# Grouped-query attention against a cache: wo in 4 KB rows, K four batches ahead from batch 20 on, a second block-diagonal P buffer in place of a ring slot

## The chip, the core and the metric

The kernel runs on one core of one Trainium2 chip. The core has a matrix engine (PE, with its weight loads listed as PEld), a vector engine (DVE), a scalar engine (ACT), a general engine (POOL), a sync engine (SP) whose only work here is to issue transfers, 16 DMA engines, an on-chip memory of 128 partitions (SBUF) and a small accumulator memory (PSUM) that the matrix engine writes. The metric is the device time of one execution in microseconds; several runs are made and the median is compared.

## What is computed

Thirty-two batches with four new tokens each attend to a cache of 2048 keys and values. There are 32 query heads over 4 key/value heads, so 8 query heads share one of K and V.

```python
B, Sq, D = 32, 4, 1024
Hq, Hkv, Sk, Dh = 32, 4, 2048, 128          # all tensors bf16
q = (x @ wq).reshape(B, Sq, Hq, Dh).transpose(0, 2, 1, 3)
k = jnp.repeat(k_cache, Hq // Hkv, axis=1)
v = jnp.repeat(v_cache, Hq // Hkv, axis=1)
scores = jnp.einsum("bhqd,bhkd->bhqk", q, k) * (Dh ** -0.5)
p = softmax(scores, axis=-1)
o = jnp.einsum("bhqk,bhkd->bhqd", p, v)
out = o.transpose(0, 2, 1, 3).reshape(B, Sq, Hq * Dh) @ wo
```

K and V of one batch are 2 MB each, wq and wo 8 MB each: some 151 MB have to be read.

## The kernel before

**Loads.** All large transfers are issued by SP, in one order written out in the code (L159 to L186): x, wq in four pieces, then K and V batch by batch, then wo in ten pieces (`WO`, in heads of 128 rows). The order of K and V is `loads` (L159): K of batches 0 to 2, then for each batch b K of b+3 (`LEAD`) and V of b. A transfer is 2 MB, 16 KB for each partition. They go round a ring of eight slots of 2 MB (`big`, `NS`): a load waits until the load that had its slot eight places before has been used up, that is until the last quarter of its K is transposed (`kt`, chunk 3) or its P*V is done (`pv`). wo goes into four slots of the same ring after the last V, in rows of 2 KB, and each of its pieces waits for its slot in the same way. SP waits in order: what is behind a waiting issue waits too.

**The projection** (L199 to L242) makes Q for all batches and leaves it transposed in `QT_sb`.

**One iteration i of the loop** (L367 to L386) writes, for each engine, its work in program order:

- POOL, `qd` (L254): the queries of batch i+1 are put on a block diagonal, `QD_sb`, four copies.
- DVE, `kt` (L263): K of batch i+1 is transposed in four chunks, two before and two after the maximum of batch i.
- PE, `pe_qk` (L271): 16 matmuls of 512 columns make the scores of batch i in `ps_s`, the one score buffer. They wait for the exp of batch i-1, which reads that buffer.
- DVE, `softmax_max` (L288): the row maximum and its negative. ACT, `softmax_exp` (L293): exp into `P_sb`, with the row sums.
- PE and ACT, `pe_ot` and `ot_evac` (L331, L336) of batch i-3: the scaled output of a batch is transposed by one matmul against the identity and copied to `oT_sb`, which shares its place with `QT_sb`; the heads of a token lie side by side there.
- DVE, `pt` (L299): P is transposed into one of two buffers `PT_sb`.
- PE, `pe_pv` (L317), 64 matmuls, and ACT, `o_evac` (L326): P*V of batch i-2 and its scaling by the inverse row sum.
- POOL, `pd` (L308): P of batch i-1 is put on a block diagonal in `PD_sb` by four copies of 32 partitions. There is one such buffer, so these copies wait for P*V of the batch before. At the end a second one, `PE_sb`, is made out of a buffer of transposed K that is no longer used; ACT zeroes it in iteration 30 (L378), it takes batch 30, and three of the four copies of batch 31 are done by DVE.

After the loop come P*V of batches 30 and 31 with what follows them, then the output product `oproj` (L344): 64 matmuls over wo's heads, in the order of its ten pieces, all of them behind the last `ot_evac`, and the copy and store of the result.

**Order around the change.** Every engine works through its own list in order, with waits on the other engines' counters. PE's list in iteration i is: scores of i, output transpose, P*V of i-2. So a P*V that waits for its V holds back the scores of the next batch.

In the profile, line L16 is the helper that issues a matmul with weights already loaded; such rows belong to the scores, to the projection or to the output product by their tile names.

Of the kernel before, what the change touches and what calls it, by code (L numbers as in the profile page):

```python
# [78 lines left out]
def bass_standalone__gqa_block_cached__sampling_kernel(  # L79
# [21 lines left out]
    NW = 4  # L101
    LEAD = 3
    NC = D // 2
    WO = (4, 4, 4, 4, 4, 4, 4, 2, 1, 1)
# [5 lines left out]
    with ExitStack() as es:  # L110
# [8 lines left out]
        QT_sb = sbuf("QT_sb", [128, B, 2, REP, Sq, 2], BF16)  # L119
        oT_sb = QT_sb[:, :, :, :, :, :].rearrange("p b a h s w -> p (b a h s w)").rearrange("p (t h) -> p t h", h=Hq)  # L120
        QD_sb = sbuf("QD_sb", [128, 2, 2, G, 32, 2], BF16)
# [5 lines left out]
        PD_sb = sbuf("PD_sb", [128, T // 2, G, 32, 2], BF16)  # L127
        PE_sb = KT_sb[:, B % 2, :, :, :, :].rearrange("p t a r w -> p (t a r w)")
        PE_sb = PE_sb.rearrange("p (t g q w) -> p t g q w", t=T // 2, g=G, q=32)
        o_sb = sbuf("o_sb", [128, Dh], BF16)  # L130
        y_sb = sbuf("y_sb", [128, D], BF16)

# [27 lines left out]
        for b in range(B):  # L160
            loads += [("k", b + LEAD)] if b + LEAD < B else []
            loads += [("v", b)]
        slot_of = {}
        holder = {s: "w" for s in range(NW)}
        for n, (kind, b) in enumerate(loads):
            s = (NW + n) % NS
            before, holder[s], slot_of[kind, b] = holder.get(s), (kind, b), s
            waits = [] if before is None else ["qproj"] if before == "w" else [
                ("kt", before[1], NCH - 1) if before[0] == "k" else ("pv", before[1])]
            src = (k_cache if kind == "k" else v_cache)[b].rearrange("g (r t) d -> (g r) t d", r=R)  # L170
            p.dma("sp", lambda e, s=s, src=src: e.dma_start(big[:, s, :, :], src), waits, (kind, b), f"s_b{s}")
        n = len(loads)
        wo_slot = [(NW + n + c) % NS for c in range(NW)]

        def wo_at(h):
            return big[:, wo_slot[h // 8], :, :].rearrange("p t d -> p (t d)")[:, h % 8 * D:(h % 8 + 1) * D]

        h0 = 0
        for c, m in enumerate(WO):
            assert h0 // 8 == (h0 + m - 1) // 8  # L180
            kind, b = holder[wo_slot[h0 // 8]]
            dst = big[:, wo_slot[h0 // 8], :, :].rearrange("p t d -> p (t d)")[:, h0 % 8 * D:(h0 % 8 + m) * D]
            p.dma("sp", lambda e, dst=dst, h0=h0, m=m: e.dma_start(
                dst.rearrange("p (h n) -> p h n", h=m), wo[h0 * 128:(h0 + m) * 128, :].rearrange("(h p) n -> p h n", p=128)),
                [("kt", b, NCH - 1) if kind == "k" else ("pv", b)], ("wo", c), f"s_wo{c}")
# [119 lines left out]
        def pd_of(i):  # L305
            return PE_sb if i == B - 2 else PD_sb

        def pd(i):  # L308
            for g in range(G):
                rows = slice(32 * g, 32 * (g + 1))  # L310
                src = words(PT_sb[rows, i % 2, :, :, :].rearrange("p t q w -> p t (q w)"))
                dst = words(pd_of(i)[rows, :, g, :, :].rearrange("p t q w -> p t (q w)"))
                waits = [("pt", i)] + (["pe0"] if i == B - 2 else ["pd0"] + ([("pv", i - 2 if i == B - 1 else i - 1)] if i else []))
                p.op("dve" if i == B - 1 and g < 3 else "pool", lambda e, s=src, d=dst: e.tensor_copy(d, s),  # L314
                     waits, ("pd", i, g))

# [14 lines left out]
        def pe_ot(i):  # L331
            buf, waits = slot(("ot", i))
            buf = ring_of["ot", i] = buf.bitcast(BF16)
            p.op("pe", lambda e: e.transpose(buf[:, 0:128], o_sb[:, :], ident[:, :]), waits + [("o", i)], ("oT", i))  # L334

        def ot_evac(i):  # L336
            buf = ring_of["ot", i]
            p.op("act", lambda e: e.activation(  # L338
                oT_sb[:, i * Sq:(i + 1) * Sq, :].rearrange("p s h -> p h s"),
                buf[:, 0:128].rearrange("p (h s) -> p h s", s=Sq), ACT.Copy),  # L340
                [("oT", i), ("qd", i)], ("ot", i))


        def oproj(c):  # L344
            for h in range(sum(WO[:c]), sum(WO[:c + 1])):
                for j in range(2):
                    out_, lhsT, rhs = ps_s[:, NC * j:NC * (j + 1)], oT_sb[:, :, h], wo_at(h)[:, NC * j:NC * (j + 1)]
                    if j == 0:
# [17 lines left out]
        kt(0, range(NCH))  # L366
        for i in range(B):  # L367
            if i < L:
                qd(i + 1)
                kt(i + 1, (0, 1))  # L370
            pe_qk(i)
            softmax_max(i)
            if i >= 3:
                pe_ot(i - 3)
                ot_evac(i - 3)
            softmax_exp(i)
            if i == L - 1:
                p.op("act", lambda e: e.memzero(words(PE_sb.rearrange("p t g q w -> p (t g q w)"))), [("qk", i)], "pe0")  # L378
            if i < L:
                kt(i + 1, (2, 3))  # L380
            pt(i)
            if i >= 2:
                pe_pv(i - 2)
                o_evac(i - 2)
            if i >= 1:
                pd(i - 1)  # L386

        pe_pv(L - 1)
        pe_ot(L - 2)
        ot_evac(L - 2)  # L390
        o_evac(L - 1)
        pd(L)
        pe_pv(L)
        pe_ot(L - 1)
        ot_evac(L - 1)
        o_evac(L)
        pe_ot(L)
# [60 lines left out]
```

## Time and profile before

Four runs took 368.52 to 371.19 us, median 370.11. The profiled execution is the one of 371.19 us; its span, from its first to its last instruction, is 369.3 us.

| | before |
|---|---|
| median of 4 runs | 370.11 us |
| profiled execution, its span | 371.19 us, 369.3 us |
| PE busy | 281.4 us (76%) |
| DVE busy | 275.2 us (75%) |
| POOL busy | 164.1 us (44%) |
| ACT busy | 122.9 us (33%) |
| read from HBM | 151.26 MB, 410 GB/s over the span |
| mean granted PE clock | 0.953 |

How to read the page's parts: the slices divide the span into 40 equal stretches of 9.23 us, and each digit is the busy share in tenths (PEclk: the granted clock of PE in tenths of full speed). The chain of work that ended last is followed back from the last instruction; a row of it has its start in us, its duration in us, the engine, what is written and the line. A row of an engine's timeline has start, duration, engine, line, operation, what is written and read, shape and count, and in square brackets how long the engine had stood idle and what ended that. Issues of transfers are listed with the time from issue to landing.

### The profile page before, as it was taken

Reading aid. Unit: us, or ns where it says so; the run is one execution under the profiler, and the core shown is the slowest. Engines: PE = TensorE matmul, PEld = TensorE weight load, DVE = VectorE, ACT = ScalarE, POOL = GpSimd, SP = SyncE. Lnnn points to the kernel's source line nnn. Section 1 sums busy time; section 2 is a strip of 40 time slices with the busy share of each in tenths; the row PEclk is TensorE's granted clock in tenths of the full one; section 3 lists DMA queues with packets and bytes.
Section 4 is the critical chain, followed back from the end, with each engine's and each line's share of the span. In section 5 each row is a group of like instructions: output and inputs, shape, how many; then the busy total and the mean of one; then the engine's idle time right before and its main releaser. Section 6 shows DMA issues by size and latency. Waiting matters only on the chain.

```text
span 369.3 us, 5961 instructions
## 1 busy us (share of the span) xinstructions
PE 281.4 (76%) x2744; PEld 144.8 (39%) x2272; DVE 275.2 (75%) x273; ACT 122.9 (33%) x135; POOL 164.1 (44%) x262
## 2 busy tenths in 40 slices
PE   1973557888888877777888878777878777768796
PEld 1001002444444444444444455433535344455722
DVE  0029577999999999999999987898697998673300
ACT  1020112333344444444433433443143344464200
POOL 5001050555555555555554445555554655518100
PEclk9998678999999999999999989998998999989989
DMA  8999999999999999999999999999999999999991
GB/s 334 431 428 426 429 428 433 431 424 425 421 428 426 426 428 426 432 426 424 428 426 428 428 427 423 426 431 426 428 428 426 428 426 429 422 426 401 387 337 47
DMA packets 14506, 151.90 MB, mean 411 GB/s; under 512 B 1296, under 2 KB 1552, under 8 KB 5776
## 3 DMA queue, kind: packets, MB, share of 16 engines
q1 hardware_dynamic: 14336, 151.39, 97.4%
q8 instruction: 20, 0.33, 0.4%
q10 hardware_dynamic: 144, 0.13, 0.1%
q14 instruction: 6, 0.05, 0.0%
HBM read 151.26 MB, written 0.26 MB: 410 GB/s over the span
## 4 chain that ended last, share of the span: by engine, by line
DMA 34%; PE 31%; DVE 18%; ACT 8%; issue 7%; SPq 1%
DMA big<-in_v_cache_dram 29%; PE ps_s L16 18%; DVE mx L289 12%; ACT P_sb L294 7%; PE ps_s L281 6%; DMA big<-in_wq_dram 6%; PE ps_r L321 5%; DVE KT_sb L269 3%; PE ps_s L349 2%; DVE negmx L290 1%; DVE PD_sb L314 1%; DVE QT_sb L242 1%; DVE KT_sb L226 1%; SPq L156 0%; ACT QT_sb L338 0%
## 5 line engine op out<-in xcount | busy, mean ns | idle before, releaser
L314 POOL COPY PD_sb<-PT_sb 32x1024 f32<-32x1024 f32 x121 | 125.6, 1038 | 136.2 <-DVE KT_sb L269 66.5
L269 DVE STREAM_TRANSPOSE KT_sb<-big 128x1024 f32<-128x1024 f32 x128 | 150.7, 1216 | 6.4 <-DMA big<-in_k_cache_dram 6.1
L321 PE MATMUL ps_r<-big,PD_sb 128*128 128x128 bf16 x1984 | 122.1, 225 | 28.3 <-DMA big<-in_v_cache_dram 25.3
L321 PEld LDWEIGHTS ps_r<-big,PD_sb 128*128 128x128 bf16 x1984 | 117.9, 101 | 35.7 <-POOL QD_sb L260 23.1
L294 ACT ACTIVATE P_sb<-ps_s,negmx 128x2048 bf16<-128x2048 f32 x32 | 81.6, 2550 | 84.4 <-DVE negmx L290 84.4
L16 PE MATMUL ps_s<-KT_sb,QD_sb 128*128 128x512 bf16 x384 | 108.2, 390 | 0.0
L289 DVE TENSOR_REDUCE mx<-ps_s 128x1 f32<-128x2048 f32 x32 | 73.3, 2290 | 22.6 <-PE ps_s L16 22.2
L281 PE MATMUL ps_s<-KT_sb,QD_sb 128*128 128x512 bf16 x128 | 50.1, 392 | 43.9 <-ACT P_sb L294 37.7
L281 PEld LDWEIGHTS ps_s<-KT_sb,QD_sb 128*128 128x128 bf16 x128 | 12.7, 99 | 123.0 <-issue 73.9
L338 ACT ACTIVATE QT_sb<-ps_r 128x128 bf16<-128x128 bf16 x32 | 23.6, 736 | 107.2 <-PE ps_r L334 107.2
L302 DVE STREAM_TRANSPOSE PT_sb<-P_sb 128x1024 f32<-128x1024 f32 x32 | 39.9, 1245 | 14.6 <-ACT P_sb L294 14.6
L260 POOL COPY QD_sb<-QT_sb 32x64 f32<-32x64 f32 x128 | 29.4, 230 | 41.7 <-DVE QT_sb L242 25.4
L357 DVE CAST y_sb<-ps_s 128x512 bf16<-128x512 f32 x1 | 0.7, 692 | 21.4 <-PE ps_s L349 21.4
L226 DVE CAST KT_sb<-ps_r 128x512 bf16<-128x512 f32 x2 | 1.3, 686 | 20.1 <-PE ps_r L210 20.1
L328 ACT ACTIVATE o_sb<-ps_r,rinv 128x128 bf16<-128x128 f32 x32 | 11.9, 371 | 12.1 <-PE ps_r L321 12.1
L349 PE MATMUL ps_s<-big,QT_sb 128*128 128x512 bf16 x32 | 13.2, 411 | 0.9 <-ACT QT_sb L338 0.9
L16 PE MATMUL ps_s<-big,QT_sb 128*128 128x512 bf16 x32 | 13.1, 411 | 0.0
L334 PEld LDWEIGHTS ps_r<-ident,o_sb 128*128 128x128 bf16 x32 | 3.1, 96 | 23.4 <-issue 22.3
L349 PEld LDWEIGHTS ps_s<-big,QT_sb 128*128 128x128 bf16 x32 | 4.7, 146 | 11.4 <-issue 11.3
L16 PE MATMUL ps_s<-big,P_sb 128*128 128x512 bf16 x32 | 9.1, 411 | 0.0
L228 ACT ACTIVATE KT_sb<-ps_r 128x512 bf16<-128x512 f32 x2 | 1.1, 594 | 23.5 <-PE ps_r L16 23.5
L210 PEld LDWEIGHTS ps_r<-big,P_sb 128*128 128x128 bf16 x8 | 0.8, 104 | 19.7 <-issue 11.7
(30 smaller groups left out, 69.0 us busy)
## 6 DMA issues: line engine op xcount, KB each, us to landing
big<-in_k_cache_dram SPq DMA_DIRECT2D x32, 2048.0 KB, 27.8
big<-in_v_cache_dram SPq DMA_DIRECT2D x32, 2048.0 KB, 32.3
big<-in_wq_dram SPq DMA_DIRECT2D x4, 2048.0 KB, 13.9
big<-in_wo_dram SPq DMA_DIRECT2D x7, 1024.0 KB, 19.0
big<-in_wo_dram SPq DMA_DIRECT2D x1, 512.0 KB, 12.8
big<-in_wo_dram SPq DMA_DIRECT2D x2, 256.0 KB, 10.3
P_sb<-in_x_dram SPq DMA_DIRECT2D x1, 256.0 KB, 2.7
out_dram<-y_sb SPq DMA_DIRECT2D x1, 128.0 KB, 1.8
```

The lines of the kernel that those rows point to most:

```text
L16: return eng.add_instruction(mybir.InstMatmult(name=nc.get_next_instruction_name(), engine=eng.engine, start_tensor_calc=start, stop_tenso ...
L260: p.op("pool", lambda e, s=src, d=dst: e.tensor_copy(d, s), waits if g == 0 else [], ("qd", i) if g == G - 1 else None)
L269: p.op("dve", lambda e, s=src, d=dst: e.transpose(d, s), waits, ("kt", i, c))
L281: mm = lambda e, a_=(out_, lhsT, rhs), f=first, l=last: e.matmul(a_[0], lhsT=a_[1], rhs=a_[2], start=f, stop=l, skip_group_check=True)
L289: p.op("dve", lambda e: e.tensor_reduce(mx[:, i % 4:i % 4 + 1], ps_s[:, :], AX.X, ALU.max), [("qk", i)], ("mx", i))
L294: p.op("act", lambda e: e.activation(P_sb[:, :, :, :].rearrange("p t r w -> p t w r"), ps_s[:, :].rearrange("p (t w r) -> p t w r", w=2, r=R),
L302: p.op("dve", lambda e: e.transpose(dst, src), [("exp", i)] + ([("pd", i - 2, G - 1)] if i > 1 else []), ("pt", i))
L314: p.op("dve" if i == B - 1 and g < 3 else "pool", lambda e, s=src, d=dst: e.tensor_copy(d, s), waits, ("pd", i, g))
L321: p.op("pe", lambda e, t=t: e.matmul(buf[:, 0:Dh], lhsT=pd_of(i)[:, t // 2, :, :, t % 2].rearrange("p g q -> p (g q)"), rhs=big[:, slot_of ...
L328: p.op("act", lambda e: e.activation(o_sb[:, :], buf[:, 0:Dh], ACT.Copy, scale=rinv[:, i % 4:i % 4 + 1]), [("pv", i), ("rinv", i)] + ([("o ...
L338: p.op("act", lambda e: e.activation(oT_sb[:, i * Sq:(i + 1) * Sq, :].rearrange("p s h -> p h s"), buf[:, 0:128].rearrange("p (h s) -> p h ...
L349: mm = lambda e, a=(out_, lhsT, rhs), h=h: e.matmul(a[0], lhsT=a[1], rhs=a[2], start=(h == 0), stop=(h == Hq - 1), skip_group_check=True)
```

## The change

- wo is loaded in rows of 4 KB: two neighbouring rows of wo go to one partition. The output therefore has to be transposed with even and odd features apart, and the one matmul of `pe_ot` becomes four with 64 columns of weights each, into halves of the partitions; `oT_sb` becomes a buffer of its own in which the 128 tokens of a weight tile lie side by side. `y_sb`, the result before its store, moves into `P_sb`.
- `SL = 20`: when V of batch 20 is due, K of batches 23 and 24 are loaded ahead of it; from there on K of b+4 is loaded ahead of V of b. From load number 43 (K of 23) on, the ring has seven slots; the eighth, `spare`, becomes `PF_sb`, a second block-diagonal P buffer, zeroed by ACT in iteration 20.
- Batches 21, 23, ..., 31 use `PF_sb`, the others `PD_sb`, and the copies wait for the last P*V that read their buffer. All copies are on POOL.
- `SW = 24`: iteration 24 has no P*V and no output transpose; from iteration 25 on P*V is that of batch i-3. After the loop come P*V of 29, 30 and 31.

```diff
@@ -100,6 +100,8 @@
     NS = 8
     NW = 4
     LEAD = 3
+    SW = 24
+    SL = 20
     NC = D // 2
     WO = (4, 4, 4, 4, 4, 4, 4, 2, 1, 1)
     scale = float(Dh) ** -0.5
@@ -117,7 +119,7 @@
         q_sb = KT_sb[:, 1, :, :, :, :].rearrange("p t a r w -> p (t a r w)")[:, 0:Hq * Dh]
         q_sb = q_sb.rearrange("p (h a g e) -> p h a g e", h=REP, a=2, g=G)
         QT_sb = sbuf("QT_sb", [128, B, 2, REP, Sq, 2], BF16)
-        oT_sb = QT_sb[:, :, :, :, :, :].rearrange("p b a h s w -> p (b a h s w)").rearrange("p (t h) -> p t h", h=Hq)
+        oT_sb = sbuf("oT_sb", [128, Hq // 2, 2, NT], BF16)
         QD_sb = sbuf("QD_sb", [128, 2, 2, G, 32, 2], BF16)
         P_sb = sbuf("P_sb", [128, T // 2, R, 2], BF16)
         P_flat = P_sb[:, :, :, :].rearrange("p t r w -> p (t r w)")
@@ -125,10 +127,8 @@
         xT_sb = P_flat[:, D:2 * D].rearrange("p (a b) -> p a b", b=128)
         PT_sb = sbuf("PT_sb", [128, 2, T // 2, 32, 2], BF16)
         PD_sb = sbuf("PD_sb", [128, T // 2, G, 32, 2], BF16)
-        PE_sb = KT_sb[:, B % 2, :, :, :, :].rearrange("p t a r w -> p (t a r w)")
-        PE_sb = PE_sb.rearrange("p (t g q w) -> p t g q w", t=T // 2, g=G, q=32)
         o_sb = sbuf("o_sb", [128, Dh], BF16)
-        y_sb = sbuf("y_sb", [128, D], BF16)
+        y_sb = P_flat[:, D:2 * D]
 
         ident = sbuf("ident", [128, 128], BF16)
         identf = sbuf("identf", [128, 128], F32)
@@ -158,30 +158,44 @@
 
         loads = [("k", b) for b in range(LEAD)]
         for b in range(B):
-            loads += [("k", b + LEAD)] if b + LEAD < B else []
-            loads += [("v", b)]
+            ahead = [b + LEAD] if b < SL else [b + LEAD, b + LEAD + 1] if b == SL else [b + LEAD + 1]
+            loads += [("k", a) for a in ahead if a < B] + [("v", b)]
+        n_pd = loads.index(("k", SL + LEAD))
+        spare = (NW + n_pd) % NS
+        pd_holder = loads[n_pd - NS]
+
+        def ring_slot(n):
+            if n < n_pd:
+                return (NW + n) % NS
+            return (spare + 1 + (n - n_pd) % (NS - 1)) % NS
+
+        PF_sb = big[:, spare, :, :].rearrange("p t d -> p (t d)").rearrange("p (t g q w) -> p t g q w", t=T // 2, g=G, q=32)
         slot_of = {}
         holder = {s: "w" for s in range(NW)}
         for n, (kind, b) in enumerate(loads):
-            s = (NW + n) % NS
+            s = ring_slot(n)
             before, holder[s], slot_of[kind, b] = holder.get(s), (kind, b), s
             waits = [] if before is None else ["qproj"] if before == "w" else [
                 ("kt", before[1], NCH - 1) if before[0] == "k" else ("pv", before[1])]
             src = (k_cache if kind == "k" else v_cache)[b].rearrange("g (r t) d -> (g r) t d", r=R)
             p.dma("sp", lambda e, s=s, src=src: e.dma_start(big[:, s, :, :], src), waits, (kind, b), f"s_b{s}")
         n = len(loads)
-        wo_slot = [(NW + n + c) % NS for c in range(NW)]
-
-        def wo_at(h):
-            return big[:, wo_slot[h // 8], :, :].rearrange("p t d -> p (t d)")[:, h % 8 * D:(h % 8 + 1) * D]
-
+        wo_slot = [ring_slot(n + c) for c in range(NW)]
+
+        def wo_at(h, m):
+            return big[:, wo_slot[h // 8], :, :].rearrange("p t d -> p (t d)")[:, h % 8 * D:(h % 8 + m) * D]
+
+        wo_v = wo.rearrange("(h p e) n -> p h (e n)", p=128, e=2)
         h0 = 0
         for c, m in enumerate(WO):
             assert h0 // 8 == (h0 + m - 1) // 8
             kind, b = holder[wo_slot[h0 // 8]]
-            dst = big[:, wo_slot[h0 // 8], :, :].rearrange("p t d -> p (t d)")[:, h0 % 8 * D:(h0 % 8 + m) * D]
-            p.dma("sp", lambda e, dst=dst, h0=h0, m=m: e.dma_start(
-                dst.rearrange("p (h n) -> p h n", h=m), wo[h0 * 128:(h0 + m) * 128, :].rearrange("(h p) n -> p h n", p=128)),
+            if m > 1:
+                dst = wo_at(h0, m).rearrange("p (h n) -> p h n", n=2 * D)
+                src = wo_v[:, h0 // 2:(h0 + m) // 2, :]
+            else:
+                dst, src = wo_at(h0, 1), wo_v[:, h0 // 2, h0 % 2 * D:(h0 % 2 + 1) * D]
+            p.dma("sp", lambda e, dst=dst, src=src: e.dma_start(dst, src),
                 [("kt", b, NCH - 1) if kind == "k" else ("pv", b)], ("wo", c), f"s_wo{c}")
             h0 += m
         assert h0 == Hq
@@ -303,16 +317,16 @@
             p.op("dve", lambda e: e.reciprocal(rinv[:, i % 4:i % 4 + 1], ssum[:, i % 4:i % 4 + 1]), [("exp", i)], ("rinv", i))
 
         def pd_of(i):
-            return PE_sb if i == B - 2 else PD_sb
+            return PF_sb if i > SL and i % 2 else PD_sb
 
         def pd(i):
+            free = [j for j in range(i) if pd_of(j) is pd_of(i)]
+            free = ("pv", free[-1]) if free else "pd0" if pd_of(i) is PD_sb else "pf0"
             for g in range(G):
                 rows = slice(32 * g, 32 * (g + 1))
                 src = words(PT_sb[rows, i % 2, :, :, :].rearrange("p t q w -> p t (q w)"))
                 dst = words(pd_of(i)[rows, :, g, :, :].rearrange("p t q w -> p t (q w)"))
-                waits = [("pt", i)] + (["pe0"] if i == B - 2 else ["pd0"] + ([("pv", i - 2 if i == B - 1 else i - 1)] if i else []))
-                p.op("dve" if i == B - 1 and g < 3 else "pool", lambda e, s=src, d=dst: e.tensor_copy(d, s),
-                     waits, ("pd", i, g))
+                p.op("pool", lambda e, s=src, d=dst: e.tensor_copy(d, s), [("pt", i), free], ("pd", i, g))
 
         def pe_pv(i):
             buf, waits = slot(("o", i))
@@ -330,21 +344,26 @@
 
         def pe_ot(i):
             buf, waits = slot(("ot", i))
-            buf = ring_of["ot", i] = buf.bitcast(BF16)
-            p.op("pe", lambda e: e.transpose(buf[:, 0:128], o_sb[:, :], ident[:, :]), waits + [("o", i)], ("oT", i))
+            ring_of["ot", i] = buf
+            for e_ in range(2):
+                for u in range(2):
+                    out_ = buf[64 * u:64 * (u + 1), 64 * e_:64 * (e_ + 1)]
+                    lhsT = o_sb.rearrange("p (d e) -> p e d", e=2)[:, e_, :]
+                    rhs = ident.rearrange("p (h u s) -> p u h s", u=2, s=Sq)[:, u, :, :]
+                    p.op("pe", lambda e, a=(out_, lhsT, rhs): e.matmul(a[0], lhsT=a[1], rhs=a[2], start=True, stop=True),
+                         waits + [("o", i)] if e_ == u == 0 else [], ("oT", i) if e_ == u == 1 else None)
 
         def ot_evac(i):
             buf = ring_of["ot", i]
             p.op("act", lambda e: e.activation(
-                oT_sb[:, i * Sq:(i + 1) * Sq, :].rearrange("p s h -> p h s"),
-                buf[:, 0:128].rearrange("p (h s) -> p h s", s=Sq), ACT.Copy),
-                [("oT", i), ("qd", i)], ("ot", i))
-
+                oT_sb[:, :, :, i * Sq:(i + 1) * Sq].rearrange("p h e s -> p e h s"),
+                buf[:, 0:128].rearrange("p (e h s) -> p e h s", e=2, s=Sq), ACT.Copy),
+                [("oT", i)], ("ot", i))
 
         def oproj(c):
             for h in range(sum(WO[:c]), sum(WO[:c + 1])):
                 for j in range(2):
-                    out_, lhsT, rhs = ps_s[:, NC * j:NC * (j + 1)], oT_sb[:, :, h], wo_at(h)[:, NC * j:NC * (j + 1)]
+                    out_, lhsT, rhs = ps_s[:, NC * j:NC * (j + 1)], oT_sb[:, h // 2, h % 2, :], wo_at(h, 1)[:, NC * j:NC * (j + 1)]
                     if j == 0:
                         mm = lambda e, a=(out_, lhsT, rhs), h=h: e.matmul(
                             a[0], lhsT=a[1], rhs=a[2], start=(h == 0), stop=(h == Hq - 1), skip_group_check=True)
@@ -365,35 +384,34 @@
         qd(0)
         kt(0, range(NCH))
         for i in range(B):
+            j = i - 2 if i < SW else i - 3 if i > SW else -1
             if i < L:
                 qd(i + 1)
                 kt(i + 1, (0, 1))
             pe_qk(i)
             softmax_max(i)
-            if i >= 3:
-                pe_ot(i - 3)
-                ot_evac(i - 3)
+            if j > 0:
+                pe_ot(j - 1)
+                ot_evac(j - 1)
             softmax_exp(i)
-            if i == L - 1:
-                p.op("act", lambda e: e.memzero(words(PE_sb.rearrange("p t g q w -> p (t g q w)"))), [("qk", i)], "pe0")
+            if i == SL:
+                p.op("act", lambda e: e.memzero(words(PF_sb.rearrange("p t g q w -> p (t g q w)"))),
+                     [("kt", pd_holder[1], NCH - 1) if pd_holder[0] == "k" else ("pv", pd_holder[1])], "pf0")
             if i < L:
                 kt(i + 1, (2, 3))
             pt(i)
-            if i >= 2:
-                pe_pv(i - 2)
-                o_evac(i - 2)
-            if i >= 1:
+            if j >= 0:
+                pe_pv(j)
+                o_evac(j)
+            if i > 0:
                 pd(i - 1)
 
-        pe_pv(L - 1)
-        pe_ot(L - 2)
-        ot_evac(L - 2)
-        o_evac(L - 1)
         pd(L)
-        pe_pv(L)
-        pe_ot(L - 1)
-        ot_evac(L - 1)
-        o_evac(L)
+        for j in range(L - 2, L + 1):
+            pe_pv(j)
+            pe_ot(j - 1)
+            ot_evac(j - 1)
+            o_evac(j)
         pe_ot(L)
         ot_evac(L)
         for c in range(len(WO)):
```

## The prediction

> **What bounds the kernel now.** I read the page's slices first, then the chain of work that ended last, then each engine's timeline around it.
>
> ```profile
> PEclk9998678999999999999999989998998999989989
> DMA  8999999999999999999999999999999999999991
> GB/s 334 431 428 426 429 428 433 431 424 425 421 428 426 426 428 426 432 426 424 428 426 428 428 427 423 426 431 426 428 428 426 428 426 429 422 426 401 387 337 47
> ```
>
> The transfer queue is full for nearly the whole span, at about 427 GB/s, a 2 MB load every 4.9 us and an iteration's two loads every 9.8. The drop to 387 comes with wo in its 2 KB rows. So time can only be won after the last load. The chain shows two regimes ahead of that:
>
> ```profile
> 188.05 2.30 DVE mx L289
> 190.56 1.14 ACT P_sb L294
> 191.70 1.27 issue
> 193.29 0.38 PE ps_s L281
> ...
> 326.42 5.36 PE ps_r L321 x64
> 331.99 0.65 PE ps_s L16 x3
> ...
> 337.80 2.29 ACT P_sb L294
> ...
> 341.72 0.67 DVE PD_sb L314
> ...
> 344.62 3.75 PE ps_r L321 x64
> 348.70 0.60 ACT o_sb L328
> 349.61 0.73 ACT QT_sb L338
> 350.48 0.41 PE ps_s L349
> ```
>
> Up to about 197 us the scores, maximum and exp of one batch follow those of the last (one ps_s): scores to maximum 3.67, to exp 2.51, to the next scores 2.76 (the timelines from 193.29 to 202.23), 8.93 us an iteration. Later P*V waits for V, and the next scores queue behind it on PE. At the end the scores of batch 31 stand behind P*V of 28, which waits for v28; then maximum, exp, transpose, the diagonal copies, P*V of 31, output product. From PE's timeline:
>
> ```profile
> 326.42 5.36 PE L321 MATMUL ps_r<-big,PD_sb 128*128 128x128 bf16 x64 [4.09 <-DMA big<-in_v_cache_dram]
> ...
> 336.28 3.75 PE L321 MATMUL ps_r<-big,PD_sb 128*128 128x128 bf16 x64 [0.98 <-POOL PD_sb L314]
> 340.75 3.75 PE L321 MATMUL ps_r<-big,KT_sb 128*128 128x128 bf16 x64 [0.73 <-POOL KT_sb L314]
> ```
>
> The first row is at half clock for part of its time: 5.36 instead of 3.73, a drop worth 1.63 us. The output product from 350.48 waits for no wo: issue times plus times to landing put wo's last piece at 352.2+10.2 = 362.4, and its last head starts near 365.4. That is 3.0 us of cover. It is PE's work, 64 matmuls at 0.215 us, with one drop (351.4 to 354.7).
>
> **When loads land.** Issue plus time to landing gives, by place in the order of loads (counted from 0): 43 at 241.5, 44 at 246.4, 45 at 251.3, 46 at 256.2, 47 at 261.1, and on by 4.9 to 57 at 310.0 and 58 at 314.9; 59 at 321.4, 60 at 326.2, about 331 and 336, and v31 (63) at 340.9. The bytes stay the same, so I keep each place's time and change what lands there: v20 moves from place 44 to 45, v21 from 46 to 47, v27 from 58 to 59, k31 from 59 to 58; v28 to v31 keep their places.
>
> **wo by 4 KB rows.** A MB lands every 2.7 us now; K and V, in 16 KB rows, take 2.45. So the 8 MB land between 0 and 2.0 us earlier; I take 1. None of it is on the path while the cover holds: 0. The Trainium skill ("DMA: Bandwidth & Descriptors", Specifications) puts line rate at 512 B and over. By it the term is 0 in any case; the trace's 387 against 427 speaks against the page.
>
> **Seven slots instead of eight.** From load 43 on a load reuses the slot of seven loads before. Counting releases along the new order (below), the tightest are v23, issued when K of 24 is transposed (265.2) and due at 280.7, a lead of 15.5 us, and v24 (274.0 for 290.5). The shortest lead in the trace is 15.2 us, in slices at full rate. Some 11 us of earlier loads still stand in the queue then. Cost 0. SP issues in order, so k28, behind v23, is held until 265.2 as well; it has until 285.6.
>
> **Zeroing the new P buffer** takes 3.6 us on ACT (row L378) and moves from iteration 30 to 20, behind its exp, at about 231 to 234.6. Queued behind it is the scaling of batch 18's output, then that batch's small transpose on PE, which stands ahead of P*V of 19; that waits for its V until 236.76 anyway: 0. In iteration 30 it hid too: 0.
>
> **Output transpose.** One 128x128 matmul becomes four half-wide ones in each batch. Low end: packed like P*V's (64 in 3.63 us, 0.057 each), 0.17 more. High end: four lone ones at 0.22 (row L334), 0.66 more. I take 0.17, the row of a dense run with changing weights, as these are. In the loop PE has room: 3.53+0.22+3.73 of 8.93 us. The copy after it (0.74 now) lies between 0.37 (row L328, dense writes) and 0.74; I take 0.6. The contiguous weights of the output product (146 ns at stride 32, others 98) lie beneath two matmuls of 0.215: 0.
>
> **The order.** Iteration 22 still has P*V of 20, but v20 now lands at 251.3 instead of 246.4. Scores of 22 start at 240.33 and end near 244.0, so PE stands 7 us. P*V follows with a drop: 5.2 us from such a P*V to the next scores (326.42 to 331.61). Scores of 23: 251.4+5.2 = 256.6 (250.13 before). P*V of 21 waits for 261.1, done at 264.8; scores of 24 by the chain at 256.6+8.93 = 265.5 (261.33 before).
>
> Iteration 24 has neither P*V nor output transpose. PE stands from about 269.2 to 274.4, over 5 us. After 4.09 the trace shows a drop; after 1.95 to 2.54 it shows one in some cases and none in others. So I charge one, 1.63 us, now in the scores of 25, which the chain runs through: scores of 26 at 274.4+8.93+1.63 = 285.0. The Trainium skill ("TensorE: Matmul & The Clock Gate", Part 1) has the clock halve after an idle window of about 3.4 us; by it the drop is sure, by the rows likely.
>
> From there the chain, at 8.93, is later than the loads: scores of 31 at 285.0+5*8.93 = 329.6. V alone would allow 321.4+3.6 = 325.0. So 2.0 us are won against 331.61 before.
>
> They are given back. P*V of 28, formerly ahead of these scores, is behind them: 329.6+3.53+0.17 = 333.3. The diagonal copy of batch 30 goes into the buffer that P*V of 28 reads, and starts when it ends: +3.86 (row pairs 207.41 and 211.27) = 337.2. Four copies on POOL, 4.48 to the next four (331.90 and 336.38), give 341.6; batch 31's four stand behind them in order, all on POOL (three were on DVE, 2.85 us), +4.37 to P*V: 346.0, against 344.62. P*V of 29 and 30, at 337 and 341.7, hide beside POOL; v31 landed at 340.9. So the late thing after V is POOL, by 5 us.
>
> **Sum.** +1.4 at P*V of 31. Behind it the transposes of 30 and 31 add 0.17 each, and the copy gives back about 0.1: +1.6. The output product keeps its 15.7 us and its drop; last wo at some 361.4 against a last head near 367. Span 369.3+1.6 = 370.9, the execution 371.19+1.6 = 372.8. That execution is 1.1 above the median of the four runs, 370.11, so I forecast 371.7, +0.4%, within the 1% that a measurement of this kernel can about tell from no change: **no change**.
>
> **Rivals.**
> - *No drop in iteration 24.* The chain is 1.63 earlier: 370.1. For it: of idle times near 2.5 us, some stay at full clock. Against: this one is twice that. A missing drop in the output product instead gives the same. 0.20.
> - *Faster: the end is bound by V, not POOL.* If neither drop nor chain holds the scores of 31 back, they start at 325.0, P*V of 31 at 341.4, 3.2 before 344.62; plus 0.2: 367.1. Without the drop in the output product 365.5, about where wo's landing (361.4 to 362.4, and 3.8 for the last head and the output) stops it. For it: V does set the chain from 202 us on. Against: the late v20 and v21, and two sets of copies behind P*V of 28. 0.13.
> - *Slower: seven slots starve the queue.* Place: v23 and v24, which wait for K of 24 and 25. If releases come later than the 11 us of queued loads, every later landing moves by the rest, wo last. It decides once that is over 4.6 us (3.0 of cover and the 1.6 of the sum): a release 16 us, two iterations, later than I count, or a queue that needs twice its backlog to stay full. Then one load's time, 4.9 us, over the forecast: 376.6. For it: leads halve from some 31 to 16. Against: 15.2 at full rate. 0.07.
> - *The change not doing what it says* would be wo by larger rows alone, if the buffer swap changed no order: 0 gain at 370.1, inside the first rival.
>
> **How the numbers follow.** Forecast 0.60 (0.10 of it with one more drop or transposes at their high end, 373.4 to 375), first rival 0.20, faster 0.13 (half of it under 366.4), slower 0.07. Below 367.1 lie some 0.1, above 374 some 0.1: range 367.1 to 374.0. Faster by over 1%: 0.07; slower by over 1%, past 373.8: 0.07 and 0.10 of the forecast's upper part: 0.17; within: 0.76.
>
> **What would show it.** P*V of 20 waits near 251 us and is 5.2 long; a PE hole of 5 us near 270 with scores of 25 at half clock; scores of 31 near 329.6; POOL busy without a hole from 337 to 346; P*V of 31 near 346, released by POOL; wo's last piece landed before its use; GB/s at 427 through 260 to 300 us. Wrong, if V's landings move by more than 3 us, if PE's clock stays up, or if POOL is not the last releaser of P*V of 31.

## The result and the profile after

The changed kernel takes 371.24 us (median of 43 runs, 369.98 to 372.55) against 369.66 us (64 runs, 368.13 to 372.17) for the kernel before: ratio 1.0035, 95% interval 1.0023 to 1.0046. It is slower by a third of a per cent, where +0.4% was forecast. The profiled execution has a span of 370.5 us, against 369.3. Both profiled executions, of 372.37 and 371.19 us, lie above their medians, so the clock drops read from them need not have the same size in every execution.

The page's slices of the changed kernel, as shown for before:

```profile
PEclk9999666999999999999999999896978999999999
DMA  8999999999999999999999999999999999999960
GB/s 333 430 426 432 430 428 430 426 421 427 427 428 428 430 424 424 429 426 426 428 428 424 424 431 425 428 426 424 426 426 432 424 428 432 424 423 410 408 271 28
```

The transfers are still at 427 GB/s up to wo, and wo itself now comes at 408 instead of 387. From 200 us on the clock dips to 8 tenths at 232 us, to 6 at 250 to 259 and to 7 and 8 from 269 to 287; before, it had five dips to 8, at 212, 249, 277, 323 and 351 us, and the last two of these are gone.

The chain of work that ended last, after (start, duration, engine, what is written, line; rows left out):

```profile
221.06 30.25 DMA big<-in_v_cache_dram
251.45 6.42 PE ps_r L335 x64
...
272.80 2.57 ACT P_sb L308 x2
275.50 0.59 PE ps_s L295
...
281.87 2.30 DVE mx L303
...
335.51 3.69 PE ps_r L335 x64
339.32 1.04 POOL PD_sb L329
...
343.79 1.04 POOL big L329
...
348.17 3.75 PE ps_r L335 x64
```

Before, transfers of V were in this chain up to 326 us. Now V is in it for the last time at 251 us; from there on it is one unbroken chain of scores, maximum and exp, and then P*V and POOL's copies. PE's timeline after shows the same places with what they waited for:

```profile
251.45 6.42 PE L335 MATMUL ps_r<-big,PD_sb 128*128 128x128 bf16 x64 [5.74 <-DMA big<-in_v_cache_dram]
...
275.50 0.59 PE L295 MATMUL ps_s<-KT_sb,QD_sb 128*128 128x512 bf16 x1 [5.25 <-ACT P_sb L308]
...
331.70 0.38 PE L295 MATMUL ps_s<-KT_sb,QD_sb 128*128 128x512 bf16 x1 [1.43 <-ACT P_sb L308]
...
335.45 3.75 PE L335 MATMUL ps_r<-big,PD_sb 128*128 128x128 bf16 x64
339.03 3.74 PE L335 MATMUL ps_r<-big 128*128 128x128 bf16 x64
342.70 0.25 PE L353 MATMUL ps_r<-ident,o_sb 128*64 128x64 bf16 x4
343.69 3.75 PE L335 MATMUL ps_r<-big,PD_sb 128*128 128x128 bf16 x64 [0.75 <-POOL PD_sb L329]
...
348.17 3.75 PE L335 MATMUL ps_r<-big 128*128 128x128 bf16 x64 [0.55 <-POOL big L329]
...
353.45 0.38 PE L368 MATMUL ps_s<-big,oT_sb 128*128 128x512 bf16 x1 [0.46 <-ACT oT_sb L358]
```

The first row is P*V of 20, waiting for its V, which now lands behind K of 24. The second is the first matmul of the scores of 25, after a standstill of 5.25 us. The third is the scores of 31: they begin at 331.70, and before at 331.61, so nothing at all is won there. Behind them stand four P*V (28 to 31) instead of three, and the last begins at 348.17 instead of 344.62. The output product begins at 353.45 instead of 350.48, but needs 14.0 us instead of 15.7, so of 3.0 us lost 1.2 remain in the span.

### The profile page after: what moved, and what is told of

Its sections match the earlier page's. It is cut to its first block, busy times and chain, and to the rows that moved or that the text cites. A ratio compares the mean times of both kernels' runs of the same rounds, so it can differ in the third digit from the quotient of the medians.

```text
span 370.5 us, 6116 instructions
## 1 busy us (share of the span) xinstructions
PE 287.3 (78%) x2840; PEld 142.6 (38%) x2368; DVE 271.8 (73%) x270; ACT 107.7 (29%) x135; POOL 166.7 (45%) x265
## 4 chain that ended last, share of the span: by engine, by line
PE 39%; DVE 22%; ACT 19%; DMA 14%; POOL 2%; issue 2%; SPq 1%; POOLq 0%
PE ps_s L16 24%; ACT P_sb L308 19%; DVE mx L303 17%; PE ps_s L295 9%; DMA big<-in_v_cache_dram 8%; DMA big<-in_wq_dram 6%; PE ps_r L335 4%; PE ps_s L368 2%; DVE KT_sb L283 2%; DVE negmx L304 1%; POOL PD_sb L329 1%; POOL big L329 1%; DVE QT_sb L256 1%; DVE KT_sb L240 1%; SPq L156 0%
## 5 line engine op out<-in xcount | busy, mean ns | idle before, releaser
L329 POOL COPY PD_sb<-PT_sb 32x1024 f32<-32x1024 f32 x104 | 107.5, 1034 | 121.7 <-PE ps_r L335 98.5
L335 PE MATMUL ps_r<-big,PD_sb 128*128 128x128 bf16 x1664 | 101.6, 224 | 12.4 <-DMA big<-in_v_cache_dram 11.6
L16 PE MATMUL ps_s<-KT_sb,QD_sb 128*128 128x512 bf16 x384 | 110.9, 398 | 0.0
L335 PEld LDWEIGHTS ps_r<-big,PD_sb 128*128 128x128 bf16 x1664 | 97.4, 100 | 14.5 <-POOL QD_sb L274 6.2
L295 PE MATMUL ps_s<-KT_sb,QD_sb 128*128 128x512 bf16 x128 | 51.5, 402 | 56.2 <-ACT P_sb L308 50.1
L358 ACT ACTIVATE oT_sb<-ps_r 128x128 bf16<-128x128 f32 x32 | 8.9, 277 | 114.3 <-PE ps_r L353 114.3
L329 POOL COPY big<-PT_sb 32x1024 f32<-32x1024 f32 x24 | 24.8, 1034 | 16.0 <-PE ps_r L335 10.3
L335 PE MATMUL ps_r<-big 128*128 128x128 bf16 x384 | 22.5, 219 | 0.5 <-POOL big L329 0.5
L335 PEld LDWEIGHTS ps_r<-big 128*128 128x128 bf16 x384 | 21.5, 98 | 0.8 <-POOL big L329 0.7
L353 PEld LDWEIGHTS ps_r<-ident,o_sb 128*64 128x64 bf16 x128 | 4.6, 108 | 31.5 <-issue 29.4
L368 PE MATMUL ps_s<-big,oT_sb 128*128 128x512 bf16 x32 | 12.1, 379 | 0.5 <-ACT oT_sb L358 0.5
L16 PE MATMUL ps_s<-big,oT_sb 128*128 128x512 bf16 x32 | 12.1, 379 | 0.0
```

Of the source, the lines that this page charges most:

```text
L16: return eng.add_instruction(mybir.InstMatmult(name=nc.get_next_instruction_name(), engine=eng.engine, start_tensor_calc=start, stop_tenso ...
L295: mm = lambda e, a_=(out_, lhsT, rhs), f=first, l=last: e.matmul(a_[0], lhsT=a_[1], rhs=a_[2], start=f, stop=l, skip_group_check=True)
L329: p.op("pool", lambda e, s=src, d=dst: e.tensor_copy(d, s), [("pt", i), free], ("pd", i, g))
L335: p.op("pe", lambda e, t=t: e.matmul(buf[:, 0:Dh], lhsT=pd_of(i)[:, t // 2, :, :, t % 2].rearrange("p g q -> p (g q)"), rhs=big[:, slot_of ...
L358: p.op("act", lambda e: e.activation(oT_sb[:, :, :, i * Sq:(i + 1) * Sq].rearrange("p h e s -> p e h s"), buf[:, 0:128].rearrange("p (e h ...
L368: mm = lambda e, a=(out_, lhsT, rhs), h=h: e.matmul(a[0], lhsT=a[1], rhs=a[2], start=(h == 0), stop=(h == Hq - 1), skip_group_check=True)
```

## The experiments

**What was to be told apart.** Theory: the new order costs time, through the wait for V of 20, the hole in iteration 24 and the clock drops behind both; the layout of wo and of the transposed output is nearly free. Rivals: the ring of seven starves the transfers; the layout costs; the order of loads costs wherever the gap stands; POOL's copies are the bound. All kernels below compute the whole result; the ratios are to the kernel before, run on the same chip. The medians come from several chips, so kernels of different rows are better compared by their ratios.

| kernel | median, us | ratio, 95% interval |
|---|---|---|
| layout alone | 367.73; again 367.62 | 0.993 (0.9904 to 0.9955); 0.9942 (0.9919 to 0.9966) |
| order alone | 371.52 | 1.005 (1.0026 to 1.0074) |
| changed kernel (both) | 371.24 | 1.0035 (1.0023 to 1.0046) |
| seven slots alone | 369.26 | 0.9983 (0.9955 to 1.0011) |
| changed, hole in 24 filled | 369.31 | 0.9975 (0.9953 to 0.9996) |
| changed, gap at 22 | 367.44; again 367.38 | 0.9953 (0.9935 to 0.997); 0.9929 (0.9905 to 0.9952) |
| changed, copies of 31 on DVE | 371.38 | 1.0026 (1.0002 to 1.0051) |
| changed, both of these | 367.42 | 0.9952 (0.9933 to 0.9971) |
| before, contiguous oT_sb alone | 368.32 | 0.9963 (0.9943 to 0.9983) |
| before, tail filled | 369.05 | 0.9984 (0.9964 to 1.0004) |

### Seven slots alone

```diff
-            s = (NW + n) % NS
+            s = ring_slot(n)      # seven slots from load 43 on, order of loads as before
```

> The kernel before with a ring of seven slots from load 43 on and nothing else; the freed slot stays empty. Theory: queue depth is not what costs, since leads of 15 us keep the transfers at full rate; GB/s stays at 427 in all slices up to wo, ratio 1.000. Rival (the queue starves): GB/s shows holes after 260 us, V of 28 lands later than 326.2, ratio 1.005 or more.

The ratio does not differ from 1, and V of 28 lands as before. From PE's timeline of this kernel, P*V of 28:

```profile
326.25 6.23 PE L329 MATMUL ps_r<-big,PD_sb 128*128 128x128 bf16 x64 [3.80 <-DMA big<-in_v_cache_dram]
```

Starvation is out. In the changed kernel leads went down to 13.6 us from issue to landing (38.3 the longest), with the slices still at full rate.

### The hole in iteration 24 filled

```diff
+            if i == SW:
+                pe_fill(80)       # 80 matmuls ident x ident into a free PSUM slot
             softmax_exp(i)
```

> The changed kernel with 80 matmuls of the identity with itself (4.5 us at full clock, results unused) on PE in iteration 24, where it stood idle for 5.25 us. Theory: the scores of 25 then run at full clock, 2.7 us shorter, and everything on the chain behind them comes 2.7 us earlier: scores of 31 at 329.0 instead of 331.7, last P*V at 345.5 instead of 348.2; time 371.2 - 2.7 = 368.5, ratio about 0.997. Rival (V or POOL set the end by themselves, the clock only fills slack): last P*V stays within 0.5 us, ratio stays at 1.0035.

The median fell by 1.9 us (371.24 to 369.31; by the ratios 0.6%, some 2.2 us), less than 2.7, but the two ratios' intervals lie apart. Engines by stretch, first the changed kernel, then this one. A row has the stretch, its length, the busy time of PE, PEld, DVE, ACT and POOL (instructions in brackets), the granted clock of PE, the DMA share and GB/s:

```profile
275.00:278.00 3.00, 2.50 (x6) 0.25 (x2) 2.65 (x5) 0.36 (x2) 0.00 (x0) 0.50 1.03 437
278.00:281.00 3.00, 3.00 (x8) 0.29 (x2) 0.95 (x1) 0.00 (x0) 0.00 (x0) 0.50 0.99 421
281.00:284.00 3.00, 3.00 (x45) 2.20 (x42) 2.13 (x1) 0.28 (x1) 0.00 (x0) 1.00 0.98 415
```

```profile
275.00:278.00 3.00, 3.00 (x21) 0.54 (x11) 2.79 (x5) 0.09 (x1) 0.00 (x0) 1.00 1.02 431
```

After the standstill PE ran at half clock for over 5 us, so that scores to maximum took 6.37 us (275.50 to 281.87) instead of 3.67; with the hole filled the clock is full. The drop is shown, and that it lies on the chain. PE's timeline of the filled kernel has P*V of 20 and the last P*V:

```profile
251.31 5.05 PE L335 MATMUL ps_r<-big,PD_sb 128*128 128x128 bf16 x64 [5.67 <-DMA big<-in_v_cache_dram]
...
344.01 3.75 PE L335 MATMUL ps_r<-big 128*128 128x128 bf16 x64 [0.55 <-POOL big L329]
```

The last P*V begins 4.2 us earlier than in the changed kernel's profile, but only 2.7 of that are the filled hole: P*V of 20 behind the same wait lost 1.3 us here and 2.7 there. Drops in one place differ in size from execution to execution, which may be why the medians differ by less than 2.7.

The Trainium skill ("TensorE: Matmul & The Clock Gate", Part 1) has the clock fall to half after at least one idle window of about 3.4 us and rise after at least one busy one. The fall after 5.25 us agrees, but in the kernel before P*V of 23 has a drop after only 1.95 us (5.36 us, at 275.92); and half clock lasted longer than one such window here, some 5.4 us (2.70 lost at half rate, doubled).

### The gap moved to iteration 22

```diff
-    SW = 24
+    SW = 22
```

> The changed kernel with the iteration that has no P*V moved from 24 to 22, where V of 20 comes late in the new order of loads. Theory: PE no longer waits for V of 20 ahead of the scores of 23. These start by the chain near 250.8 instead of 257.7, with the one clock drop of 2.7 us in them; scores of 31 then start near 325.3, bound by V of 27 (321.4 + 3.75), not 331.7; the last P*V near 342 instead of 348.2, and the end is set by the last landing of wo (361.3) or the output product, span near 365 to 366: ratio about 0.990 to 0.993. Rival (the order of loads, not the place of the gap, is what costs): the wait of 5.7 us for V of 20 moves to iteration 23 whole, ratio stays at 1.002 or more.

By the medians 3.8 us are won against the changed kernel; by the ratios it is 0.8%, some 3.0 us (3.9 in the repeat below). PE's timeline of this kernel has the drop in the scores of 23 now and P*V of 20 directly behind them without a wait. P*V of 27 waits 1.10 us for its V, and the scores of 31 begin close behind it, at 325.41 instead of 331.70:

```profile
249.17 0.59 PE L295 MATMUL ps_s<-KT_sb,QD_sb 128*128 128x512 bf16 x1 [5.26 <-ACT P_sb L308]
...
254.72 3.75 PE L335 MATMUL ps_r<-big,PD_sb 128*128 128x128 bf16 x64
...
321.38 3.75 PE L335 MATMUL ps_r<-big 128*128 128x128 bf16 x64 [1.10 <-DMA big<-in_v_cache_dram]
...
341.87 3.75 PE L335 MATMUL ps_r<-big 128*128 128x128 bf16 x64 [0.55 <-POOL big L329]
...
358.78 0.39 PE L368 MATMUL ps_s<-big,oT_sb 128*128 128x512 bf16 x1 [0.56 <-DMA big<-in_wo_dram]
```

The last P*V is 6.3 us earlier than in the changed kernel (341.87 for 348.17), but the last row shows the output product waiting for wo. So the order of loads is not to blame, the place of the gap is. V of 20, pushed behind K of 24, is first missed in iteration 22; the gap came in 24, and PE had stood 5.7 us for that V by then. The gap at 22 was run with the new layout only.

### Three copies of batch 31 on DVE

```diff
-                p.op("pool", lambda e, s=src, d=dst: e.tensor_copy(d, s), [("pt", i), free], ("pd", i, g))
+                p.op("dve" if i == B - 1 and g < 3 else "pool", lambda e, s=src, d=dst: e.tensor_copy(d, s), [("pt", i), free], ("pd", i, g))
```

> The changed kernel with three of the four diagonal copies of batch 31 back on DVE, beside POOL's copies of batch 30. Theory: POOL's queue of two sets is the last thing ahead of the final P*V; batch 31's copies now wait for its transposed P and for P*V of 29 (about 342.7) instead, take 2.9 us on DVE, and the last P*V starts near 345.8 instead of 348.2: ratio about 0.997 to 0.998. Rival (DVE and POOL copies slow each other, as the rows of 1.42 and 1.56 us in the kernel before hint): 0.5 us or less is won, ratio 1.002 or more.

The rival's figure came, but not for its reason. The three copies took 3.47 us on DVE (2.85 in the kernel before) and were done in time, at 346.55; what was late was P*V of 30, which stands ahead on PE. From PE's timeline:

```profile
343.91 3.75 PE L335 MATMUL ps_r<-big,PD_sb 128*128 128x128 bf16 x64 [0.75 <-POOL PD_sb L329]
347.58 0.25 PE L353 MATMUL ps_r<-ident,o_sb 128*64 128x64 bf16 x4
347.77 3.75 PE L335 MATMUL ps_r<-big 128*128 128x128 bf16 x64
```

P*V of 31 follows that of 30 without a wait, 12.1 us behind the P*V of 28 at 335.66, instead of 12.7. So batch 31's copies on POOL cost 0.6 us between these two profiles, too little to tell in the medians (371.38 and 371.24). P*V of 30 waits 0.75 us for POOL's copies of batch 30 in both. The bulk is PE's own: one more P*V of 3.6 us behind the scores of 31.

### Both

> As the last, with three copies of batch 31 on DVE as well. Theory: with POOL's queue shortened the last P*V is bound by the landing of V of 31, 341.0, some 1 us earlier than without; the end then waits for wo's last landing, so at most 0.5 us more is won than by the gap's place alone: ratio 0.989 to 0.993. Rival (POOL is the bound even then): 2 us more.

367.42 against 367.44: nothing more is won, as expected where wo's landing ends the kernel.

### Layout alone

The kernel before with the wo rows, the four matmuls of `pe_ot`, the new `oT_sb` and its copy from the change, and nothing of the order.

> The kernel before with the wo part of the change alone: 4 KB rows, four half-wide matmuls for the output transpose, the new oT_sb. Theory: it is nearly free. The copy of the transposed output takes 0.277 us in the changed kernel instead of 0.738, and from the start of the last P*V to the output product it is 5.28 us instead of 5.86; the four matmuls add 0.22 us behind the scores. Wo's faster landing lies under the output product. So about 0.5 us less than before: ratio 0.999. Rival (the layout is what costs): four lone matmuls on the way to each P*V, +0.66 us three times in the tail, ratio 1.003 to 1.005.

Both theory and rival missed: it wins 1.9 us, four times what was expected. PE's timeline has the last P*V, the transposes of 30 and 31 and the second head of the output product:

```profile
342.95 3.75 PE L325 MATMUL ps_r<-big,PD_sb 128*128 128x128 bf16 x64
346.63 0.25 PE L343 MATMUL ps_r<-ident,o_sb 128*64 128x64 bf16 x4
347.51 0.25 PE L343 MATMUL ps_r<-ident,o_sb 128*64 128x64 bf16 x4 [0.63 <-ACT o_sb L332]
348.65 0.38 PE L358 MATMUL ps_s<-big,oT_sb 128*128 128x512 bf16 x1
```

From the last P*V to the output product it is 5.3 us (5.86 before; the first matmul of the product left no record and is put 0.43 us ahead of the last row), and heads follow each other by 0.43 us from the first: there is no drop in the product. That profile's lead over before at the last P*V (342.95 for 344.62) is no gain of the layout: P*V of 28 happened to have no drop either, and that is worth 1.63 us.

### Which part of the layout

In the kernel before, the copy of the transposed output writes single elements 64 bytes apart (0.738 us); with the new buffer it writes runs of four (0.277). The next kernel changes only that.

```diff
+        oT_sb = sbuf("oT_sb", [128, Hq, NT], BF16)
...
-                oT_sb[:, i * Sq:(i + 1) * Sq, :].rearrange("p s h -> p h s"),
+                oT_sb[:, :, i * Sq:(i + 1) * Sq],
```

> The kernel before with only the buffer of the transposed output changed, so that the 128 tokens of a weight tile lie side by side; wo stays in 2 KB rows and the output transpose one matmul. Theory: the gain of the layout is the end of the tail, not wo's rows: shorter copies (0.74 to some 0.3 us) and no clock drop in the output product, since the standstill ahead of it is shorter. So the same as with the whole layout, ratio 0.993 to 0.995, unless wo's last landing (362.4) stops it, 0.995 then. Rival (the four plain matmuls keep the clock up, where a transpose does not count): the drop stays in some executions, ratio 0.998 to 0.999.

The ratio lies between the two figures: 1.1 us are won, with wo in 2 KB rows and one matmul for the transpose, and again without the drop. The output product then waits for wo:

```profile
357.16 0.39 PE L349 MATMUL ps_s<-big,oT_sb 128*128 128x512 bf16 x1 [0.49 <-DMA big<-in_wo_dram]
...
362.93 0.38 PE L16 MATMUL ps_s<-big,oT_sb 128*128 128x512 bf16 x1
```

Wo's last piece, in 2 KB rows, is issued at 352.1 and lands 10.1 later, at 362.2; with 4 KB rows it lands at 346.6+14.7 = 361.3. So the larger rows can bring 0.9 us, and only once the product is early enough to wait. The medians, 368.32 against 367.6 or 367.7, fit that, but the intervals of the ratios overlap.

### The drop in the output product

```diff
         pe_ot(L - 1)
+        pe_fill(14, 0)
...
         pe_ot(L)
+        pe_fill(14, 1)
```

> The kernel before with twice 14 matmuls of the identity with itself (0.8 us each, results unused) on PE after P*V of 31, ahead of and behind the last output transpose, where it stood. Theory: the drop in the output product comes from the standstill, so it goes: product 14.0 instead of 15.7 us, ratio 0.996 to 0.998 (executions without the drop win nothing). Rival (the drop comes from the strided weights or from the clock's own course): the product stays at 15.7 in the profile and the ratio at 1.000.

In the kernel before, stretches of the output product ran at these granted clocks (0.75 and 0.68), and with the filled tail at those of the second list (1.00):

```profile
350.00:353.00 3.00, 2.52 (x9) 0.75 (x5) 0.00 (x0) 0.34 (x1) 0.00 (x0) 0.75 1.05 386
353.00:356.00 3.00, 3.00 (x11) 0.74 (x5) 0.00 (x0) 0.00 (x0) 0.00 (x0) 0.68 1.06 388
```

```profile
350.00:353.00 3.00, 2.62 (x13) 1.03 (x7) 0.00 (x0) 0.04 (x1) 0.00 (x0) 1.00 1.05 386
353.00:356.00 3.00, 3.00 (x15) 1.00 (x7) 0.00 (x0) 0.00 (x0) 0.00 (x0) 1.00 1.05 385
```

The median ratio alone, 0.9984 with 1 in its interval, would not decide it. The spread does: of 64 runs of the kernel before 28 lie over 370.3 us, with none between 369.96 and 370.72, and of the 29 made beside this kernel 10 lie over 370.3; of 12 with the filled tail none does, nor of the 12 with the contiguous buffer and the 21 with the whole layout. That the upper group is the executions with the drop is read from profiles: those of the kernel before (371.19 us) and of the seven slots (371.89) lie in it and have the drop, this one (369.10) has none. The weights were strided and the transpose a single one here as before, so neither makes the drop by itself. It goes with the standstill of some 2 us and costs 1.7 us.

### Order alone

The changed kernel with wo, `pe_ot`, `oT_sb` and its copy as before.

> The changed kernel with wo, the output transpose and oT_sb as before: the order of loads, the seven slots, the second P buffer and P*V three behind, alone. Theory: the order costs and the layout wins, and the change is their sum. The layout alone won 2 to 2.6 us, so the order alone should lose that more than the changed kernel: 371.2 + 2.3 = 373.5, ratio 1.008 to 1.012, with the clock drop back in the output product (15.7 us instead of 14.0). Rival (the two parts do not add, since the tail of the new order hides the drop): ratio 1.002 to 1.005.

The rival held: 1.005, and in the one profiled execution (372.44 us) no drop in the product even with the old layout. Its first row on record (the second matmul) and its last:

```profile
353.79 0.38 PE L16 MATMUL ps_s<-big,QT_sb 128*128 128x512 bf16 x1 [1.15 <-ACT QT_sb L348]
...
367.17 0.38 PE L16 MATMUL ps_s<-big,QT_sb 128*128 128x512 bf16 x1
```

That is 13.4 us at full clock. So the parts do not add: 0.993 times 1.005 would be 0.998, and the changed kernel has 1.0035. Under the old order the layout gains by sparing a drop and part of a standstill; under the new one, if the profile is typical, there was no drop left to spare. How often the product has none there, and why the clock stays up with the same standstill ahead of it, was not tried; in that order four P*V run nearly without a break before it.

### Layout alone and the gap at 22, side by side

> The layout alone once more, beside the next kernel on one chip. Theory: both end with the last landing of wo and are equal to 0.1%: ratio 0.994 to 0.995, and the order of loads brings nothing that the layout has not brought. Rival (the order with its gap at 22 wins by itself): the next kernel is faster than this one by 0.3% or more.

> The changed kernel with its gap at 22 once more, beside the layout alone on one chip. Theory: as that one, ratio 0.994 to 0.995, with a narrower spread, since P*V of 31 is done some 1 us earlier and wo's landing alone sets the end. Rival: 0.991 or less.

367.62 and 367.38 us, with overlapping intervals. Both beat the kernel before by some 2 us (369.48 on this chip) and the changed kernel by some 4. The order with its gap in the right place has the narrower spread (367.26 to 367.62 against 367.21 to 368.62). In its profile the output product waits for wo (0.59 us), in that of the layout alone no such wait shows, which fits an end set by wo's landing alone; that it holds in the other executions is not shown. In the median it is 0.2 us ahead of the layout, which the intervals do not tell from nothing.

## Why the prediction was right, point by point

- **No change, 371.7 us:** right: 371.24, +1.6 us or 0.43% on the medians, +1.2 us in the two profiled spans, against +1.6 forecast. Three of its terms were mis-sized and cancelled in the profiles, so that the number came out this close is partly luck; the places of the losses were foreseen.
- **Loads keep their places in time:** right. P*V of 20 began at 251.45 (251.4 forecast), and V of 31 landed at 322.3+18.7 = 341.0 (340.9).
- **Seven slots cost nothing, zeroing costs nothing:** right, by the run with seven slots and by ACT's timeline, where the zeroing stood at 229.9 to 233.5 and the next P*V waited for V anyway (2.39 us, at 236.77).
- **The clock drops:** right in place, wrong in size. Each was charged 1.63 us, read from the row of 5.36 us. Scores of 25 lost 2.70; P*V of 20 took 6.26 us to the next scores, where 5.2 was forecast. Together 2.1 us more in this profile: scores of 31 at 331.70, not 329.6, and the 2.0 us that were to be won there came to nothing.
- **The gain given back behind the scores of 31:** right in sum (16.47 us from the scores to the last P*V, 16.4 forecast), half right in its reason. POOL was the last releaser of P*V of 31, as named, and kept the forecast distances (335.45, 339.32, 343.79, 348.17). But the step let P*V of 29 and 30 hide beside POOL, and the copies on DVE showed that P*V of 30 ends only 0.6 us ahead of it. It is PE's list, one more P*V, that is long: without batch 31's copies on POOL it is 0.6 us shorter.
- **Output transpose and its copy:** the four matmuls added 0.22 us (0.17 forecast). The copy took 0.277 us, below the low end of 0.37, and from the last P*V to the product it is 5.28 us where 5.86 plus 0.2 was forecast: 0.8 us better.
- **"The output product keeps its 15.7 us and its drop":** wrong, 14.0 us. This term, -1.7, and the -0.8 before it cancelled the +2.1 of the two larger drops.
- **wo by 4 KB rows, 0 on the path, 1 us in landing:** right for this kernel: the last piece lands at 361.3 (361.4 forecast), 5 us ahead of its use. The trace's 408 against 387 GB/s in 2 KB rows speaks against the Trainium skill ("DMA: Bandwidth & Descriptors", Specifications), which puts line rate at 512 B and over.
- **The rivals.** The faster one described the gap's better place: last P*V at 341.4 forecast there, 341.87 measured with the gap at 22, and wo's landing as what stops it. Its price was right (367.1 named, 367.44 and 367.38 measured), and its condition was one number away in the code. The one without a drop in iteration 24 was refuted by the scores of 25; the filled hole measures its price, 369.31 us where 370.1 was named. Starvation was refuted. That larger wo rows alone would gain nothing, as the last one had it, does not hold for the whole layout, which won 1.9 us.

## What to carry to other kernels

When a software pipeline is deepened in mid-run, put the empty iteration where the input that was pushed back is first missed; a gap two iterations late costs the wait and the gap. Look for every place where PE will stand for more than some 2 us and charge the work behind it a clock drop, from 1.3 to 2.7 us here and sometimes none, but only where that work lies on the chain; filling the hole with idle matmuls is a cheap test. And take a change apart before judging it: here the layout alone was 0.6 to 0.7% faster and the order alone 0.5% slower.

## What was not expected of the hardware

- A copy on ACT of 128x128 elements out of PSUM takes 0.738 us when each element is written 64 bytes from the last and 0.277 us when runs of four are written, whether it reads F32 (changed kernel) or bf16 (contiguous buffer alone).
- Weight loads with a stride of 64 bytes take 0.144 us in the output product and contiguous ones 0.098; beneath two matmuls of 0.215 us the difference did not show in the time.
- Whether a standstill of PE is followed by a clock drop is not settled by its length alone. In the P*V rows of all profiles here from 60 us on, drops came after 1.75 us (5.36 for 3.73 us, hole filled) and stayed out after 3.49 us (layout alone); every standstill of 3.8 us or more had one.
- Nor does the length settle the size: 1.63 us in many rows (P*V of 5.36 us), 1.3 after 5.67 us (5.05), 2.5 after 3.80 us (6.23), 2.7 after 5.74 us (6.42). The scores of 23 behind the gap at 22 lost 1.8 us in one profile and 2.6 in its repeat, after 5.26 and 5.27 us.
